# The mean of squares of eight head pairs: from TensorE to VectorE's transposes and sums

## The chip, the cores and the metric

One core of a Trainium2 chip runs the kernel. The time is device time in microseconds (us) of one execution; lower is better. TensorE (PE) does matrix products, VectorE (DVE) and ScalarE (ACT) element-wise work, GpSimd (POOL) almost nothing here, SyncE (SP) starts most transfers. Each engine works through its own queue in order and waits on semaphores where it needs another's result.

## The reference

An attention block without softmax feeds a two-layer network. Everything is float32 in and out.

```python
kv  = np.einsum('bhsd,bhse->bhde', k, v)            # 8 batches, 8 heads, 576 tokens, head size 64
out = np.einsum('bhsd,bhde->bhse', q, kv)
rms = np.sqrt(np.mean(out * out, axis=-1, keepdims=True) + 1e-06)
x   = (out / rms * g_norm)                          # then (b, s, h*d): 4608 tokens x 512
h   = x @ w_in                                      # 512 x 2048
g   = h * erf(softplus(h))
y   = g @ w_out                                     # 2048 x 512
```

The part that matters here is `np.mean(out * out, axis=-1)`: the mean over the 64 values of one head of one token.

## The kernel before, in words

The tokens are worked in nine groups of 512, T = 0 to 8. Group T below 8 holds the first 512 tokens of batch T; the 64 tokens that are left of each batch are collected in `x_last` and make the ninth group. A group's attention is worked in four pairs of heads, p = 0 to 3: two heads of 64 stand above one another on the 128 partitions, tokens lie along the free axis, so a result of a pair is 128x512. The network is worked by 16 units f of 128 of its 2048 hidden values: `h` for the unit (four TensorE products with one 128x512 weight tile in plain float32, or twelve with three fp32r forms of each operand: high, low and both), softplus, erf in batches of four units, the product h·s ("gate", L1082), and the projection by `w_out`.

**Three ways to do the norm.** The mean runs over partitions, which no element-wise engine sums. In the group T = 0 (`first_group`, L873) TensorE sums it with `mean_w`, a matrix with 1/64 in two 64x64 blocks. The groups T = 1 and T = 2 (`attention`, L404) do so too, and this is what the change touches. The pair (1,0) does it with two float32 products (L476). The other seven pairs first halve the squares into two fp32r numbers on VectorE (`halve`: L459 and L460) and make four fp32r products (L470, L471). Logarithm, exponential and square (L482 to L484) then give 1/rms on ScalarE, on 128x512 elements, since the products write the mean to all 64 rows of a head; VectorE adds a correction step (L490, L493) and multiplies the attention result by it (L502). The groups from T = 3 on (`paired`, L542) do two pairs at once and use no TensorE for it: VectorE transposes the squares in blocks of 32x32 (L629), so that 32 rows come to lie along the free axis, and sums them (L630). Each head then has two partial sums on different partitions. Four ScalarE copies (`across`, L643) bring each to the other's place, VectorE adds them (L644), logarithm, exponential and square run on 128x32 elements (L649 to L651), two small operations correct (L658, L661), and a transpose with a broadcast input (L665) spreads the result over 128x512 again.

**What sets the order.** The program is written under a manual schedule: each engine takes its instructions in the order in which Python issues them. The first group has a list of names (ORDER). Then a loop (L1156) runs over n = 0 to 32, units f of the groups T = 0 and T = 1; in it stand, at each step, the weight tiles still to be made from 64-bit inputs (`weights`, L309: ScalarE converts the lower halves, L271, VectorE does four operations, L281 to L292, the last of which writes the tile), the gate product of an earlier unit (L1175 or L1220), the hidden product of unit n, its evacuation from PSUM by ScalarE (L1214 for float32, L1216 for the fp32r forms, where VectorE adds the second bank, L753), its softplus (L1230) and the projection of the unit n-5 (L834). While the group T is in the network, the attention of the group T+1 is done a piece at a time. `pieces_of` (L1028) puts these pieces into four lists for each step f; the loop calls list 3 and list 0 ahead of the step's hidden product, list 1 after its softplus, list 2 at the end of the step. With T+1 = 1 the pairs begin at steps n = 3, 6, 9 and 12, with T+1 = 2 at n = 16, 20, 24 and 28; `halve` and the copies of the kept tail (`keep_tail`, L447: the 64 last tokens and the next pair's kv) run two steps later in list 3, `mean` in that step's list 1 (list 2 for pair (1,0)), `norm` one step later in list 0. The last pair, (2,3), has its `mean` and `norm` after the loop, in `held_sums` (L1110). While the group T = 1 is in the network, the weights are also split into three fp32r forms (L737, L740, L743) and written to DRAM, and the last four units' gated values are split into `g_held` (L713, L716, L719) for products at L1098. A second loop (L1323) does the remaining seven groups in fp32r, with the weight forms read back from DRAM (`w_in_parts`, `w_out_parts`).

PSUM: two banks (`ps_h`) take hidden products in turn, four (`ps_o`) the projections, and `at_ps` two banks the attention pieces of a pair.

Of the kernel before, what the change touches and what calls it, by code (L numbers as in the profile page):

```python
# [39 lines left out]
FP32 = mybir.dt.float32  # L40
# [8 lines left out]
EPS = 1e-6  # L49
# [21 lines left out]
def kernel(  # L71
# [41 lines left out]
    def exp_ln_table():  # L113
        nc.scalar.preload_act_table_set("natural_log_exp_and_others")
# [225 lines left out]
    def qt_tile(name):  # L340
        return attp.tile([P, S], FP32, name=name, tag="qT", bufs=2)
# [58 lines left out]
    def keep_prepared():  # L400
        kept.pop()()
        turn(1, 0)

    def attention(T, p):  # L404

        st = {}

        halves = T > 1 or (T == 1 and p > 0)
        then = divmod(T * NP + p + 1, NP)
        both = (T, p) == (FIRST, NP - 1)  # L410
        more_cols = slice(kv_cols.stop, kv_cols.stop + D)

        two = halves_of

        bd = kv_of(T, p)

        def square_tile(name):
            return qt_tile(name)[:, 0:G]

        def visit():  # L420


            qT = ready.pop((T, p))
            at = st["at"] = at_tile()
            x = halves_of(qT[:, 0:G])
            for a, i in ((0, 0), (0, 1), (1, 0), (1, 1)):
                nc.tensor.matmul(  # L427
                    at[rows_of[i if a else 1 - i], a, 0 : 2 * P],
                    lhsT=bd[rows_of[i], a * D : (a + 1) * D],
                    rhs=x[rows_of[i], a],  # L430
                    start=True,
                    stop=True,
                )
            for s in rows_of:
                nc.tensor.matmul(
                    at[s, 1, 2 * P : 2 * P + R], lhsT=bd[s, D : 2 * D], rhs=qT[s, G:S], start=True, stop=True
                )
            st["o"] = at[:, :, 0 : 2 * P]
            for _, product_ in kv_products(*then, at[:, 1, kv_cols], at[:, 0, kv_cols], first=1):
                product_()  # L440
            if both:
                for _, product_ in kv_products(then[0], 1, at[:, 1, more_cols], at[:, 0, more_cols]):
                    product_()
            st["sq"] = qT[:, 0:G]
            nc.scalar.activation(two(st["sq"]), st["o"], AF.Square)

        def keep_tail():  # L447
            nc.vector.tensor_copy(
# [3 lines left out]
            if both:  # L452
                kv_kept(then[0], 1, st["at"], more_cols)

        def halve():
            sq = st.pop("sq")
            hi = st["hi"] = attp.tile([P, G], FP32R, name="sq_hi", tag="rms_r")
            lo = st["lo"] = attp.tile([P, G], FP32R, name="sq_lo", tag="sq_lo")
            nc.vector.tensor_copy(out=hi, in_=sq)  # L459
            nc.vector.tensor_tensor(out=lo, in0=sq, in1=hi.bitcast(FP32), op=ALU.subtract)  # L460

        def mean(table=True):
            ms = st["ms"] = st["at"][:, :, 2 * P : 4 * P]
            parts = [(ms[:, a], a) for a in range(2)]
            if halves:


                hi, lo = two(st.pop("hi")), two(st.pop("lo"))
                for ps, a in parts:
                    nc.tensor.matmul(ps, lhsT=mean_w, rhs=hi[:, a], start=True, stop=False)  # L470
                    nc.tensor.matmul(ps, lhsT=mean_w, rhs=lo[:, a], start=False, stop=True)  # L471
                u = square_tile("u")
            else:
                u = st.pop("sq")
                for ps, a in parts:
                    nc.tensor.matmul(  # L476
                        ps, lhsT=mean_w.bitcast(FP32), rhs=two(u)[:, a], start=True, stop=True
                    )
            r = attp.tile([P, G], FP32, name="rms_r", tag="rms_r")
            exp_ln_table()  # L480
            st["u"], st["r"] = u, r
            nc.scalar.activation(two(r), ms, AF.Ln, bias=eps_col)  # L482
            nc.scalar.activation(r, r, AF.Exp, scale=-0.5)
            nc.scalar.activation(u, r, AF.Square)  # L484
            if table:
                softplus_table()

        def norm():
            ms, u, r = (st.pop(name) for name in ("ms", "u", "r"))
            nc.vector.scalar_tensor_tensor(  # L490
                out=two(u), in0=ms, scalar=EPS, in1=two(u), op0=ALU.add, op1=ALU.mult
            )
            nc.vector.scalar_tensor_tensor(  # L493
                out=u, in0=u, scalar=3.0, in1=r, op0=ALU.subtract, op1=ALU.mult
            )
            if T < FIRST:
                if T not in xT:
                    xT[T] = wide.tile([P, KC, G], FP32, name="xT", tag="ab"[T])
                x = xT[T][:, p, :]
            else:  # L500
                x = st["x"] = x_new.tile([P, G], FP32, name="x", tag="x")
            nc.vector.scalar_tensor_tensor(  # L502
                out=two(x),
                in0=st.pop("o"),
                scalar=gm_col,
                in1=two(u),
                op0=ALU.mult,
                op1=ALU.mult,
            )
# [23 lines left out]

        first_ = (partial(prepare, T, p),) if (T, p) == (1, 0) else ()
        then_ = partial(turn, *then)
        pieces = (first_, (visit, loads), (halve, keep_tail) if halves else (keep_tail,))
        return (*(partial(chain, *group) for group in pieces), mean, partial(chain, norm, then_), split)


    twice = {}  # L540

    def paired(T, p):  # L542
# [73 lines left out]
                twice["o", n] = o  # L616
                nc.scalar.activation(x, o, AF.Square, scale=0.125)

        def small(name):
            t = twice[name] = attp.tile([P, 2 * BLOCKS], FP32, name=name, tag=name)  # L620
            return t

        def block_sums():


            total = small("ms")
            for n in range(2):
                t = attp.tile([P, G], FP32, name="sq_t", tag=("rms_r", "sq_lo")[n])
                nc.vector.transpose(out=t, in_=twice["x"][n])  # L629
                nc.vector.tensor_reduce(  # L630
                    out=total[:, n * BLOCKS : n * BLOCKS + BLOCKS],
                    in_=t.rearrange("p (c d) -> p c d", c=BLOCKS),
                    axis=AX.X,
                    op=ALU.add,
                )

        def across():


            total, other = twice["ms"], small("ms_other")  # L640
            for n in range(4):
                rows, beside = (slice(32 * k, 32 * k + 32) for k in (n, n ^ 1))
                nc.scalar.copy(other[rows], total[beside])  # L643
            nc.vector.tensor_tensor(out=total, in0=total, in1=other, op=ALU.add)  # L644

        def root():
            total, r, u = twice["ms"], small("rms"), small("rms_u")
            exp_ln_table()
            nc.scalar.activation(r, total, AF.Ln, bias=eps_col)  # L649
            nc.scalar.activation(r, r, AF.Exp, scale=-0.5)  # L650
            nc.scalar.activation(u, r, AF.Square)  # L651
            softplus_table()

        def spread():


            total, r, u = (twice[name] for name in ("ms", "rms", "rms_u"))
            nc.vector.scalar_tensor_tensor(  # L658
                out=u, in0=total, scalar=EPS, in1=u, op0=ALU.add, op1=ALU.mult
            )  # L660
            nc.vector.scalar_tensor_tensor(  # L661
                out=u, in0=u, scalar=3.0, in1=r, op0=ALU.subtract, op1=ALU.mult
            )
            for n in range(2):
                nc.vector.transpose(  # L665
                    out=twice["x"][n].rearrange("p (c d) -> p c d", c=BLOCKS),
                    in_=u[:, n * BLOCKS : n * BLOCKS + BLOCKS].unsqueeze(2).to_broadcast([P, BLOCKS, 32]),
                )

        def norm(n):  # L670
            x = twice["x"][n]
# [356 lines left out]
    def pieces_of(T):  # L1028


        steps = [([], [], [], []) for _ in range(FC)]
        for p in range(NP):
            products, apply, halve, mean, norm, split = attention(T, p)
            f = (BATCH - 1) * (p + 1) if T < FIRST else BATCH * p

            steps[f][2 if T == FIRST or p == 1 else 1].append(products)
            if T < FIRST and p == 0:
                steps[f + 2][3].append(apply)
            else:
                steps[f + 1][1].append(apply)  # L1040
            steps[f + 2][3].append(halve)
            with_erf = (f + 2) % BATCH == BATCH - 1

            place = 2 if T < FIRST and p == 0 else 1
            if T == FIRST and p == NP - 1:
                ending.extend((partial(mean, table=False), norm, split))
                continue
            steps[f + 2][place].append(partial(mean, table=not with_erf))
            steps[f + 3][0].append(norm)
            steps[min(f + 4, FC - 1)][0].append(split)  # L1050
        return steps
# [400 lines left out]
```

## Time and profile before

| | |
|---|---|
| three runs: median (lowest to highest) | 885.0 us (884.7 to 885.28) |
| the profiled execution: time | 885.01 us |
| its span | 883.2 us |
| TensorE clock granted | 1.0 |
| ScalarE, busy share of the span | 63% |
| DMA, mean rate over the span | 294 GB/s |
| attention pieces of T = 1 lie from about | 41 us to 122 us |
| those of T = 2 from about | 134 us to 231 us |

The profile shows one execution. Its page lists the busy time of each engine and, in 40 equal slices of the span, the busy share in tenths. Further views of the same trace are the chain of waits (for each moment, what the work that ended last was waiting for), the timeline (start, duration, engine, line, operation and tile, and in brackets how long the engine stood idle before it and for whom), busy times of the engines in a stretch, and the durations of all instructions of a line (lowest/median/highest in ns, first and last start).

### The profile page before, as it was taken

Reading aid. Unit: us, or ns where it says so; the run is one execution under the profiler, and the core shown is the slowest. Engines: PE = TensorE matmul, PEld = TensorE weight load, DVE = VectorE, ACT = ScalarE, POOL = GpSimd, SP = SyncE. Lnnn points to the kernel's source line nnn. Section 1 sums busy time; section 2 is a strip of 40 time slices with the busy share of each in tenths; the row PEclk is TensorE's granted clock in tenths of the full one; section 3 lists DMA queues with packets and bytes.
Section 4 is the critical chain, followed back from the end, with each engine's and each line's share of the span. In section 5 each row is a group of like instructions: output and inputs, shape, how many; then the busy total and the mean of one; then the engine's idle time right before and its main releaser. Section 6 shows DMA issues by size and latency. Waiting matters only on the chain.

```text
span 883.2 us, 13286 instructions
## 1 busy us (share of the span) xinstructions
PE 875.1 (99%) x4874; PEld 659.1 (75%) x4874; DVE 752.6 (85%) x1107; ACT 559.3 (63%) x789; POOL 4.7 (1%) x14
## 2 busy tenths in 40 slices
PE   8999999999999999999999999999999999999998
PEld 4444456666788888888888888888888888888887
DVE  5889978899998898989898989898979797966667
ACT  5977677777775657565665647474757575755552
POOL 2000000000000000000000000000000000000000
PEclk9999999999999999999999999999999999999999
DMA  9977427989799997999799979998797779778871
GB/s 291 291 225 224 132 75 285 342 310 341 262 358 401 330 347 251 385 328 349 232 382 350 353 231 346 366 342 295 272 351 282 288 288 344 289 279 334 316 255 49
DMA packets 136929, 259.89 MB, mean 294 GB/s; under 512 B 78816, under 2 KB 87264, under 8 KB 136864
## 3 DMA queue, kind: packets, MB, share of 16 engines
q1 hardware_dynamic: 136128, 258.09, 82.8%
q10 hardware_dynamic: 544, 0.82, 0.3%
q8 instruction: 39, 0.64, 0.3%
q14 instruction: 26, 0.21, 0.1%
q0 software_dynamic: 192, 0.13, 0.0%
HBM read 224.40 MB, written 34.60 MB: 293 GB/s over the span
## 4 chain that ended last, share of the span: by engine, by line
PE 91%; DMA 3%; DVE 2%; ACT 2%; issue 1%; SPq 0%; DVEq 0%; ACTq 0%
PE n_ps L778 48%; PE m_ps L778 24%; PE o_ps L834 8%; PE h_ps L1201 5%; DMA w_out_parts<-w_out 1%; PE at_ps L557 1%; DMA q_sb<-in_q_dram 1%; PE off_ps L588 1%; DMA w_in<-w_new 1%; PE warm_ps L982 1%; DMA w_in_parts<-w_in 0%; PE at_ps L427 0%; ACT s_sb L1154 0%; PE at_ps L440 0%; ACT L1154 0%
## 5 line engine op out<-in xcount | busy, mean ns | idle before, releaser
L778 PE MATMUL n_ps<-w_out_parts,g_forms 128*128 128x512 f32 (+1 forms) x936 | 230.1, 388 | 0.2 <-DMA w_out_parts<-w_out 0.2
L778 PE MATMUL n_ps<-x_forms,w_in_parts 128*128 128x512 f32 x896 | 222.6, 390 | 0.0
L778 PEld LDWEIGHTS n_ps<-w_out_parts,g_forms 128*128 128x128 f32 x936 | 175.0, 188 | 36.7 <-DMA w_out_parts<-w_out 0.9
L778 PEld LDWEIGHTS n_ps<-x_forms,w_in_parts 128*128 128x128 f32 x896 | 167.4, 188 | 35.1
L753 DVE TENSOR_TENSOR h<-m_ps,h 128x512 f32<-128x512 f32 x116 | 78.5, 686 | 58.6 <-PE m_ps L778 58.5
L1358 ACT ACTIVATE h<-n_ps 128x512 f32<-128x512 f32 x112 | 66.7, 596 | 94.0 <-PE n_ps L778 91.8
L1363 ACT ACTIVATE s<-h 128x512 f32<-128x512 f32 x112 | 69.2, 632 | 88.6 <-DVE h L753 88.6
L778 PE MATMUL m_ps<-w_out_parts,g_forms 128*128 128x512 f32 x464 | 123.9, 389 | 0.0
L778 PE MATMUL m_ps<-x_forms,w_in_parts 128*128 128x512 f32 x448 | 119.7, 389 | 0.0
L778 PEld LDWEIGHTS m_ps<-w_out_parts,g_forms 128*128 128x128 f32 x464 | 87.1, 188 | 18.1
L778 PEld LDWEIGHTS m_ps<-x_forms,w_in_parts 128*128 128x128 f32 x448 | 84.1, 188 | 17.5
L753 DVE TENSOR_TENSOR e<-m_ps,e 128x512 f32<-128x512 f32 x116 | 80.1, 692 | 14.1 <-PE m_ps L778 3.4
L834 PE MATMUL o_ps<-w_out_sb,h_sb 128*128 128x512 f32 x192 | 86.8, 595 | 0.0
L713 ACT ACTIVATE g_forms<-h 128x1024 fp32r<-128x1024 f32 x58 | 60.8, 1061 | 39.2 <-PE m_ps L778 21.0
L719 DVE SCALAR_TENSOR_TENSOR g_forms<-g_forms 128x1024 fp32r<-128x1024 f32 x58 | 71.1, 1226 | 2.0
L716 DVE TENSOR_TENSOR g_forms<-h,g_forms 128x1024 fp32r<-128x1024 f32 x58 | 70.5, 1215 | 0.5 <-ACT g_forms L713 0.4
L1412 DVE TENSOR_TENSOR h<-h,s 128x1024 f32<-128x1024 f32 x56 | 65.9, 1217 | 0.0
L834 PEld LDWEIGHTS o_ps<-w_out_sb,h_sb 128*128 128x128 f32 x192 | 35.5, 190 | 38.3 <-issue 36.9
L748 DVE SCALAR_TENSOR_TENSOR e<-n_ps,e 128x512 f32<-128x512 f32 (+1 forms) x89 | 59.8, 671 | 3.4 <-PE n_ps L778 3.4
L1201 PE MATMUL h_ps<-xT,w_in_sb 128*128 128x512 f32 x128 | 57.9, 596 | 1.3 <-DVE w_in_sb L292 1.2
L117 ACT ACT_TABLE_LOAD x43 | 55.2, 1283 | 0.8
L1386 ACT ACTIVATE s<-s 128x1024 f32<-128x1024 f32 x50 | 50.6, 1054 | 0.3
(166 smaller groups left out, 936.6 us busy)
## 6 DMA issues: line engine op xcount, KB each, us to landing
w_out_parts<-w_out SPq DMA_DIRECT2D x116, 768.0 KB, 7.2
w_in_parts<-w_in SPq DMA_DIRECT2D x112, 768.0 KB, 6.7
w_in<-w_new SPq DMA_DIRECT2D x16, 768.0 KB, 4.8
k_sb<-in_k_dram SPq DMA_DIRECT2D x32, 288.0 KB, 6.1
v_sb<-in_v_dram SPq DMA_DIRECT2D x31, 288.0 KB, 5.7
w_raw<-in_moe_w_in_dram SPq DMA_DIRECT2D x16, 512.0 KB, 6.3
w_raw<-in_moe_w_out_dram SPq DMA_DIRECT2D x8, 1024.0 KB, 5.3
out_dram<-e SPq DMA_DIRECT2D x32, 256.0 KB, 4.0
```

What stands on the lines that cost most here:

```text
L117: nc.scalar.preload_act_table_set("softplus")
L713: nc.scalar.activation(high, x, AF.Copy, scale=1.0 + 2.0**-13)
L716: nc.vector.tensor_tensor(out=low, in0=x, in1=high.bitcast(FP32), op=ALU.subtract)
L719: nc.vector.scalar_tensor_tensor(out=both, in0=low.bitcast(FP32), scalar=SHIFT, in1=high.bitcast(FP32), op0=ALU.mult, op1=ALU.add,)
L748: nc.vector.scalar_tensor_tensor(out=out_, in0=ps, scalar=scale, in1=out_, op0=ALU.mult, op1=ALU.add)
L753: nc.vector.tensor_tensor(out=out_, in0=ps, in1=out_, op=ALU.add)
L778: nc.tensor.matmul(ps[:, cols], lhsT=weights(form, k), rhs=moving(form, k)[:, cols], start=(form == forms[0] and k == 0), stop=(form == fo ...
L834: nc.tensor.matmul(o_ps[j], lhsT=g[:, j * P : j * P + P], rhs=one(w_out_sb, f), start=(f == 0), stop=last,)
L1201: nc.tensor.matmul(plain[i], lhsT=blocks_of(one(w_in_sb, i % FC))[:, c], rhs=xT[T][:, c, :], start=(c == 0), stop=(c == KC - 1),)
L1358: nc.scalar.activation(h[:, i], n_ps, AF.Copy, scale=SHIFT - 1.0)
L1363: nc.scalar.activation(s[:, i], h[:, i], AF.Softplus)
L1412: nc.vector.tensor_tensor(out=part(h, half), in0=part(h, half), in1=part(s, half), op=ALU.mult)
```

## The change

In `attention` the mean goes the way that `paired` already goes. The steps of `paired` become functions that both call: `small`, `sums_of_blocks`, `meet`, `roots` and `spread_over`; for the groups from T = 3 on they issue what was issued before. For the eight pairs of T = 1 and T = 2, `halve`, the products with `mean_w`, and the three ScalarE and two VectorE operations on 128x512 go. In their place come: the transpose and the sum right behind the kept tail's copies (`block_sums`, list 3), the four copies and the add at once behind them (`across`, list 0 of the same step, so ahead of that step's hidden product and its evacuation), logarithm, exponential and square on 128x16 where `mean` stood, and two small operations, the spreading transpose and the multiplication where `norm` stood. The square takes a scale of 1/8, so that sums are means. The first group keeps its TensorE products. No transfer is added, removed or moved in SyncE's queue.

```diff
+    def sums_of_blocks(squares):
+        total = small("ms", len(squares))
+        for n, x in enumerate(squares):
+            t = attp.tile([P, G], FP32, name="sq_t", tag=("rms_r", "sq_lo")[n])
+            nc.vector.transpose(out=t, in_=x)
+            nc.vector.tensor_reduce(
+                out=total[:, n * BLOCKS : n * BLOCKS + BLOCKS],
+                in_=t.rearrange("p (c d) -> p c d", c=BLOCKS), axis=AX.X, op=ALU.add,
+            )
+        return total
+
+    def meet(total):
+        other = small("ms_other", total.shape[1] // BLOCKS)
+        for n in range(4):
+            rows, beside = (slice(32 * k, 32 * k + 32) for k in (n, n ^ 1))
+            nc.scalar.copy(other[rows], total[beside])
+        nc.vector.tensor_tensor(out=total, in0=total, in1=other, op=ALU.add)
...
     def attention(T, p):
...
-            nc.scalar.activation(two(st["sq"]), st["o"], AF.Square)
+            nc.scalar.activation(halves_of(st["sq"]), st["o"], AF.Square, scale=0.125)
...
-        def halve():
-            sq = st.pop("sq")
-            hi = st["hi"] = attp.tile([P, G], FP32R, name="sq_hi", tag="rms_r")
-            lo = st["lo"] = attp.tile([P, G], FP32R, name="sq_lo", tag="sq_lo")
-            nc.vector.tensor_copy(out=hi, in_=sq)
-            nc.vector.tensor_tensor(out=lo, in0=sq, in1=hi.bitcast(FP32), op=ALU.subtract)
-
-        def mean(table=True):
...
-                for ps, a in parts:
-                    nc.tensor.matmul(ps, lhsT=mean_w, rhs=hi[:, a], start=True, stop=False)
-                    nc.tensor.matmul(ps, lhsT=mean_w, rhs=lo[:, a], start=False, stop=True)
...
-            nc.scalar.activation(two(r), ms, AF.Ln, bias=eps_col)
-            nc.scalar.activation(r, r, AF.Exp, scale=-0.5)
-            nc.scalar.activation(u, r, AF.Square)
+        def block_sums():
+            st["ms"] = sums_of_blocks([st["sq"]])
+
+        def across():
+            meet(st["ms"])
+
+        def root(table=True):
+            st["r"] = roots(st["ms"], table)
...
-        pieces = (first_, (visit, loads), (halve, keep_tail) if halves else (keep_tail,))
-        return (*(partial(chain, *group) for group in pieces), mean, partial(chain, norm, then_), split)
+        pieces = (first_, (visit, loads), (keep_tail, block_sums), (across,))
+        return (*(partial(chain, *group) for group in pieces), root, partial(chain, norm, then_), split)
...
-            products, apply, halve, mean, norm, split = attention(T, p)
+            products, apply, keep, meets, mean, norm, split = attention(T, p)
...
-            steps[f + 2][3].append(halve)
+            steps[f + 2][3].append(keep)
+            steps[f + 2][0].append(meets)
```

## The prediction

> **What bounds the kernel now.** I began with the page's first two parts, busy time by engine and in 40 slices.
>
> ```profile
> PE 875.1 (99%) x4874; PEld 659.1 (75%) x4874; DVE 752.6 (85%) x1107; ACT 559.3 (63%) x789; POOL 4.7 (1%) x14
> ...
> PE   8999999999999999999999999999999999999998
> PEclk9999999999999999999999999999999999999999
> ```
>
> TensorE (PE) has work in 99% of the span and its clock is full in every slice. The average says that what leaves TensorE is a gain. But a gapless engine also has no slack to lend: any wait that is put in front of it is paid whole. So I read next, stage by stage, what stands just ahead of TensorE. By busy time per stretch, TensorE has 23.00 of the 23.50 us from 50.0 to 73.5, and VectorE (DVE) 22.60: there VectorE is as full as TensorE. From 73.5 to 118.4 TensorE has every microsecond, VectorE 41.80 of 44.90. The chain of waits around the first two pairs concerned (start, us, what):
>
> ```profile
> 45.73 0.22 DVE x_last L448
> ...
> 46.79 0.70 DVE w_e L281
> ...
> 49.51 1.24 DVE w_in_sb L292
> 50.74 0.04 issue
> 50.78 3.70 PE h_ps L1201 x8
> ...
> 69.59 0.12 PE at_ps L470
> 69.71 0.12 PE at_ps L471
> 69.82 0.12 PE at_ps L470
> 69.94 0.12 PE at_ps L471
> 70.06 3.43 PE o_ps L834 x8
> ```
>
> The reader is to see two things. Before 50.78 the chain runs on VectorE without a break: the kept tail of pair (1,0), then the four operations that make a weight tile, then TensorE, which the timeline shows standing still for that tile. From there on the chain is TensorE's own, and the four mean matmuls of a pair are 4 x 0.12 = 0.47 us of it.
>
> ```profile
> 50.78 3.70 PE L1201 MATMUL h_ps<-xT,w_in_sb 128*128 128x512 f32 x8 [0.50 <-DVE w_in_sb L292]
> ```
>
> **What goes.** On TensorE: seven pairs x 0.47 = 3.29 us, all of it in the gapless chain (69.59, 92.03, 114.47, 141.7, 168.5, 195.4, 222.04), and 1.03 us of L476 for pair (1,0) at 49.26. The latter stands before the 0.50 us stall above, and the stall ends when VectorE ends; it counts for nothing. On VectorE, per pair: L459 0.43, L460 0.69, L490 0.69, L493 0.69 = 2.50 (pair (1,0): 1.38). On ScalarE (ACT): L482 to L484, 0.69 + 0.63 + 0.63 = 1.95.
>
> **What comes.** The third and later groups do the same operations already, so the prices are rows of the trace:
>
> ```profile
> L643 ACT COPY ms_other<-ms x48: 213/217/219, 250.4 to 751.3; 32x32 f32<-32x32 f32 x48
> L629 DVE STREAM_TRANSPOSE sq_t<-x x24: 701/702/703, 246.4 to 747.9; 128x512 f32<-128x512 f32 x24
> L630 DVE TENSOR_REDUCE ms<-sq_t x24: 685/686/687, 247.1 to 748.7; 128x16 f32<-128x512 f32 x24
> ```
>
> VectorE: transpose 0.70, reduce 0.69, the add of the two halves 0.18 (L644), two small products 0.18 and 0.19 (L658, L661), the spreading transpose 0.69 (L665) = 2.63 per pair. In total that is no more than before (+0.13), except for pair (1,0), +1.25. ScalarE: four copies 0.90 (at 250.45, one group), then 0.32 + 0.23 + 0.23 for logarithm, exponential and square = 1.68 against 1.95. The rows for the small ones are of 128x32 and 32x32, the change has half that width: between nothing and these rows. I take the rows, since a transpose of 128x512 and a copy of 32x32, sixty-four times apart in size, differ by a factor of three only.
>
> A rule stands against cutting ScalarE's work this small: the Trainium skill, "VectorE: DVE Perf Modes", section "The TRN2 errata — SBUF-src ops pay a fixed extra latency per instruction", gives ScalarE a fixed cost of 224 cycles for each operation within SBUF and says that many small tiles pay it each. By it a 32x16 copy would be an estimated 200 ns, so four of them 0.80 us where the trace's group has 0.90; the sum would be smaller by some 0.1 us at a place where a pair waits for them.
>
> So busy time is a wash, and the order decides. Before, the squares went to TensorE and VectorE was free of the pair until the logarithm came back, several microseconds later. Now VectorE's add waits for ScalarE's copies, which wait for VectorE's reduce, and both queues run in order: behind the add stand the weight tiles and the gate products, behind the copies stands the evacuation of the hidden product's bank.
>
> **Step 1, pair (1,0).** The kept tail starts at 45.73 and ends at 46.79. Then transpose and reduce, to 48.21; ScalarE is busy with nothing that must come first after the square that ends at 45.70, so its copies run 48.25 to 49.15; the add; and L281 starts at 49.30 where it started at 46.79. The tile's join L292 ends 2.5 us later and TensorE stands for it: **+2.5**. Bounds: +1.4, if the copies cost no wait (transpose and reduce remain), and +3.0, if the two hand-overs to ScalarE and back take 0.25 each more than the 0.04 allowed here (the square's, at 45.70, took 0.03).
>
> **Step 2, pairs (1,1) to (1,3).** TensorE loses 3 x 0.47 = **-1.41**. VectorE: pair (1,1)'s copies stand in ScalarE's queue behind a batch of erf with its two table loads:
>
> ```profile
> 66.72 1.28 ACT L117 ACT_TABLE_LOAD   x1
> 68.02 1.16 ACT L271 ACTIVATE w_m<-w_raw 128x1024 int32<-128x1024 uint32 x1
> ```
>
> They come where L271 stands: 68.02, with the 2.5 us of step 1 70.5, done at 71.4. The next L281, at 65.37 before, starts at 71.57: VectorE is 6.2 us late, TensorE 2.5 - 0.47 = 2.0. The idle 0.38 ahead of L490 at 74.23 and the cheaper end of the pair (1.06 for 1.38) give back 0.7. The gate product that a projection needs ends at 81.66, the projection (L834) starts at 84.97: 3.3 us of cover against a lag of 5.5 - 2.0 = 3.5: a wait of about 0.2. Pairs (1,2) and (1,3) stall VectorE 1.0 each (four copies and two hand-overs; the add follows the reduce at once). Cover at the next two: gate 104.46, projection 107.41, 2.95; gate 123.61, projection 125.24, 1.63. By the same count 1.5 and 1.2 are waited there. Sum 2.9; none, if idle stretches of VectorE that I haven't seen pass (3.1 us of 44.9 are idle from 73.5 to 118.4) absorb it. Between 0 and 2.9 I take **+2.3**, nearer to the count, since TensorE's own shortening eats the cover too.
>
> **Step 3, pairs (2,0) to (2,2).** No stall: in these steps two weight tiles' splits (L740, L743) stand between reduce and add. The copies precede the evacuation L1216, but would end at 140.7 for a product that ends at 140.9, and with 1.3 and 0.6 us to spare at the other two. So 3 x 0.47 = **-1.41**. If they don't fit: up to +0.3 each.
>
> **Step 4, pair (2,3).** This step has no projection between two hidden products, so TensorE waits for the bank that L1216 empties:
>
> ```profile
> 218.22 0.22 DVE L448 COPY x_last<-at_ps 128x64 f32<-128x64 f32 x1
> 218.53 0.60 ACT L1216 ACTIVATE h<-n_ps 128x512 f32<-128x512 f32 x1 [0.37 <-PE n_ps L778]
> 219.25 0.42 PE L778 MATMUL n_ps<-x_high,w_new 128*128 128x512 f32 x1
> ...
> 222.90 1.18 PE L1098 MATMUL o_ps<-w_place,g_held 128*128 128x512 f32 x4 [0.23 <-DVE g_held L719]
> ```
>
> Without L459 and L460 the kept tails run from 217.15 to 219.2 (two kv sums here), transpose and reduce to 220.6, the copies to 221.5, the evacuation to 222.1: the product of L778 starts at 222.16, not 219.25, +2.9. Less the mean, 0.47, and the two later waits for g_held (0.23 and 0.15), which the delay covers: **+2.05**. Bounds: -0.47 (copies fall behind the evacuation) to +2.45.
>
> **Sum**: 2.5 - 1.41 + 2.3 - 1.41 + 2.05 = +4.0. After 225 TensorE is the chain to the end and the DMA has spare time on the whole, so the shift stays, less at most the 0.2 us that TensorE waits for w_out_parts near 242. The profiled execution took 885.01 us (span 883.2, 1.8 around it, untouched), the median of the runs shown is 885.0: **889.0 us**.
>
> **The rivals.**
> **Only the matmuls count (faster).** If the copies come through without any wait for TensorE, the gain is 3.29: 881.7. Point from which it decides: the new operations of pair (1,0) must cost VectorE under about 0.5 us before 50.7, and the last pair's copies must be out before 218.5. The tail ends at 46.79 and the tile follows without a gap, and the last pair's squares are done only at 217.1, 1.4 us ahead of the evacuation, with 0.70 + 0.69 needed before the first copy: this speaks against. For it: TensorE is 99% busy, and the work that leaves it is certain.
> **Cover holds in the middle (hardly slower).** Steps 1 and 4 cost as counted, but VectorE's lag never reaches TensorE: 2.5 - 2.82 + 2.05 = +1.7, 886.7. For it: cover of 3.3, 2.95 and 1.63 us; against: VectorE has 93% of that stretch.
> **The lag adds up (much slower).** Step 2 at its upper end 2.9, the copies of (2,0) to (2,2) past the evacuation by 0.3 each: +5.5, 890.5.
> **It does not do what it says.** The order of instructions on TensorE shows 29 rows fewer, so the matmuls do go; that the time stays at 885 by waits that happen to equal the gain needs steps 1 and 4 half as large.
>
> **How the numbers follow.** The forecast has 0.62, the large lag 0.15, the covered middle 0.12, no change by cancelling 0.04, faster 0.07. About 0.2% (1.8 us) is what a measurement of this kernel can tell from no change, so 886.7 is still "within": faster 0.07, same 0.16, slower 0.77. Range 886.4 to 890.8: it leaves out the faster case, the cancelling one and the ends of steps 1 and 3 together.
>
> **What would show it.** Right: TensorE idle of some 2.5 to 3 us ahead of h_ps near 50 to 53, put down to w_in_sb; a VectorE idle of 2 to 4 us ahead of the small add of pair (1,1); idle ahead of two or three L834 projections put down to the gate product h_sb; idle of nearly 3 us ahead of n_ps near 220. Wrong: if any of these is missing, its term goes; if TensorE's busy time does not fall by about 4 us, the gain side was misread; if the time is lost after 242, the DMA was the cause and not the queues.

## The result, and the profile after

The changed kernel takes 892.8 us (median of four executions, 892.58 to 894.54), the kernel before 885.02. The ratio is 1.0092, 95% interval [1.0075, 1.0110]: slower by 7.8 us. The forecast was slower by 4.0, and the measured time lies above the range that was given (886.4 to 890.8).

The profiled execution of the changed kernel is its slowest one: 894.54 us, span 892.7. Its first 46 us hold 0.9 us that are no part of the change: TensorE there waits 1.1 us for a query transfer (`q_sb`), before the first changed instruction; in the profiles of other kernels here that wait is absent or shorter, whatever their code. Shifts below are told with that 0.9 taken off.

The page's first two parts, as they were shown of before:

```profile
PE 874.8 (98%) x4842; PEld 656.9 (74%) x4842; DVE 754.6 (85%) x1125; ACT 556.9 (62%) x821; POOL 4.7 (1%) x14
...
PE   8989989999899999999999999999999999999998
PEclk9989999999999999999999999999999999999999
```

TensorE has 32 instructions less, and yet its busy time hardly fell, from 875.1 to 874.8. One digit gives the hint: the granted clock, all nines before, has an 8 in the third slice. Instructions that run there at a lower clock are longer, and they are counted as busy. The row is coarse: a nine stands for anything from 90% up over 22 us, and a second fall, near 230 us, doesn't change its digit. The longest of TensorE's waits, from 23 to 260 us (engine and line, what it waited for, us in total, times, longest):

```profile
PE h_ps L1180 <- ACT rms L435: 3.9, 1, 3.9
PE o_ps L812 <- DVE h_sb L1061: 2.9, 2, 1.5
PE n_ps L756 <- ACT h L1195: 2.7, 1, 2.7
```

These are the three places that the prediction named, with waits of the sizes that it named. The first, in the timeline (start, duration, engine, line, operation, in brackets the idle time before it and who ended it):

```profile
49.19 0.84 ACT L428 COPY ms_other<-ms 32x16 f32<-32x16 f32 x4 [2.56 <-DVE ms L414]
...
50.06 0.18 DVE L429 TENSOR_TENSOR ms<-ms,ms_other 128x16 f32<-128x16 f32 x1 [0.91 <-ACT ms_other L428]
50.16 0.69 DVE L281 TENSOR_SCALAR w_e<-w_raw 128x1024 f32<-128x1024 f32 x1
...
52.87 1.23 DVE L292 CUSTOM_DVE_ANT_0 w_in_sb<-w_e,w_m 128x2048 uint16<-128x2048 uint16 x1
...
54.24 6.38 PE L1180 MATMUL h_ps<-xT,w_in_sb 128*128 128x512 f32 x8 [3.89 <-ACT rms L435]
```

Two things are to be read. VectorE stands 0.91 us ahead of its add, then makes the weight tile, which is done at 54.10; TensorE starts right after. (The profile names the exponential L435 as releaser because that ended at 54.23; experiments below, with the exponential elsewhere, name `w_in_sb`; in e3_dve_copies it ended 3.4 us earlier, and the product starts 0.14 us behind the tile, as here.) And the eight products then take 6.38 us, where the same eight took 3.70 in the profile before. Busy time by stretch (stretch, length, TensorE, its weight loads, VectorE, ScalarE, GpSimd, granted clock, DMA share, GB/s):

```profile
50.00:60.00 10.00, 6.11 (x8) 2.48 (x8) 9.52 (x14) 6.75 (x10) 0.00 (x0) 0.66 0.58 185
```

The granted clock is 0.66 in the mean over these 10 us; from 60 to 78 it is 1.00 again. In steps of 0.1 us it is half from 52.86, still within the wait, to 59.68:

```profile
52.86:59.68 6.82, 5.44 (x7) 2.37 (x8) 6.54 (x9) 3.97 (x6) 0.00 (x0) 0.50 0.81 259
230.35:233.76 3.41, 3.41 (x10) 2.63 (x9) 2.67 (x5) 1.80 (x4) 0.00 (x0) 0.50 1.09 320
```

The second row belongs to the third wait, which has the same sequel:

```profile
227.65 0.84 ACT L428 COPY ms_other<-ms 32x16 f32<-32x16 f32 x4 [2.47 <-DVE ms L414]
228.52 0.60 ACT L1195 ACTIVATE h<-n_ps 128x512 f32<-128x512 f32 x1
...
229.17 0.50 PE L756 MATMUL n_ps<-x_high,w_new 128*128 128x512 f32 x1 [2.73 <-ACT h L1195]
...
230.48 0.63 PE L756 MATMUL n_ps<-x_low,w_new 128*128 128x512 f32 x1
```

The evacuation L1195 stands behind the four copies, as forecast, and TensorE behind it. One microsecond after it goes on, its products turn from 0.39 to 0.63 us. The waits of the middle stage (L812 for the gate product `h_sb`, 1.46 and 1.41 us) have no such sequel: the eight products after each take 3.70:

```profile
114.19 3.70 PE L812 MATMUL o_ps<-w_out_sb,h_sb 128*128 128x512 f32 x8 [1.46 <-DVE h_sb L1061]
...
133.03 3.70 PE L812 MATMUL o_ps<-w_out_sb,h_sb 128*128 128x512 f32 x8 [1.41 <-DVE h_sb L1061]
```

By TensorE's own starts, the shift of each stage against the profile before (0.93 taken off; each entry is the difference of two starts):

| | us |
|---|---|
| wait ahead of the product at 54.24 | +2.53 |
| its lower clock, 6.38 in place of 3.70 | +2.67 |
| means of (1,1) to (1,3) gone | -1.41 |
| waits for the gate product, 0.13 + 1.53 + 1.56 | +3.2 |
| hand-overs up to the first product of pair (2,0) | +0.53 |
| means of (2,0) to (2,2) gone | -1.46 |
| wait ahead of the product at 229.17 | +2.90 |
| its lower clock (the 12 products, from start to start: 2.79 to 4.30) | +1.51 |
| mean of (2,3), waits for g_held gone | -1.27 |
| sum, at 245 us | +9.2 |

By the end of the span 8.6 are left (892.7 - 883.2 - 0.9). The median of the four executions, 7.8, is lower still, and so is their loss of clock: the profiled one has a mean granted clock of 0.994, the other three 0.995 to 0.996.

### The profile page after: what moved, and what is told of

Its sections match the earlier page's. It is cut to its first block, busy times and chain, and to the rows that moved or that the text cites. A ratio compares the mean times of both kernels' runs of the same rounds, so it can differ in the third digit from the quotient of the medians.

```text
span 892.7 us, 13259 instructions
## 1 busy us (share of the span) xinstructions
PE 874.8 (98%) x4842; PEld 656.9 (74%) x4842; DVE 754.6 (85%) x1125; ACT 556.9 (62%) x821; POOL 4.7 (1%) x14
## 4 chain that ended last, share of the span: by engine, by line
PE 87%; DVE 5%; ACT 5%; DMA 2%; issue 1%; SPq 0%; DVEq 0%; ACTq 0%
PE n_ps L756 50%; PE m_ps L756 25%; PE o_ps L812 5%; PE h_ps L1180 3%; DVE w_e L287 1%; PE at_ps L574 1%; PE off_ps L605 1%; PE n_ps L1077 1%; DMA q_sb<-in_q_dram 1%; ACT s_sb L1133 1%; DVE w_e L284 1%; ACT L117 1%; DMA w_raw<-in_moe_w_out_dram 1%; DVE w_e L281 1%; ACT L1133 0%
## 5 line engine op out<-in xcount | busy, mean ns | idle before, releaser
L812 PE MATMUL o_ps<-w_out_sb,h_sb 128*128 128x512 f32 x192 | 87.1, 596 | 2.9 <-DVE h_sb L1061 2.9
L812 PEld LDWEIGHTS o_ps<-w_out_sb,h_sb 128*128 128x128 f32 x192 | 35.9, 190 | 43.4 <-issue 37.8
L1180 PE MATMUL h_ps<-xT,w_in_sb 128*128 128x512 f32 x128 | 60.5, 619 | 4.6 <-ACT rms L435 3.9
L1180 PEld LDWEIGHTS h_ps<-xT,w_in_sb 128*128 128x128 f32 x128 | 24.9, 198 | 37.1 <-issue 29.4
```

Source lines behind the costliest of these rows:

```text
L812: nc.tensor.matmul(o_ps[j], lhsT=g[:, j * P : j * P + P], rhs=one(w_out_sb, f), start=(f == 0), stop=last,)
L1180: nc.tensor.matmul(plain[i], lhsT=blocks_of(one(w_in_sb, i % FC))[:, c], rhs=xT[T][:, c, :], start=(c == 0), stop=(c == KC - 1),)
```

## The experiments

**Theory A**: the two long waits are what the prediction said, order and hand-overs, but each is paid a second time, since TensorE runs at a lower clock after it. **Theory B**: the clock falls there for another reason. **Theory C**: it is not the place; VectorE's and ScalarE's new work costs this time wherever it stands.

### e1_fill: the same waits, but TensorE not idle in them

```diff
+        def fills(count):
+            for n in range(count):
+                nc.tensor.matmul(
+                    st["at"][:, n % 2, 2 * P : 4 * P],
+                    lhsT=mean_w.bitcast(FP32),
+                    rhs=halves_of(st["sq"])[:, n % 2],
+                    start=True,
+                    stop=True,
+                )
...
         def root(table=True):
+            if (T, p) == (1, 0):
+                fills(6)
```

and `fills(4)` for (2,3) behind the hidden product of step 30.

> The changed kernel with idle TensorE time filled: six 128x256 float32 products with mean_w (0.51 us each by L476) go where pair (1,0) had its mean, four go behind the hidden product of step 30; they write the unused part of at_ps, their result is read by nothing. No wait of VectorE or ScalarE is touched. Theory A (each of the two long waits is paid twice, once as a wait and once because TensorE's clock is lower after it): h_ps at 54.24 takes 3.7 instead of 6.38 us and the products after 229.17 go at full clock; 892.8 - 2.7 - 1.7 = 888.4, and the remaining waits of TensorE are as long as before less the fill. Theory B (the clock is low there for another reason, such as the power of VectorE's work): 892.8 as before, both clock dips stay. If the fill is longer than the wait: above 888.4 by the excess.

889.31 us; 885.31 before on the same chip; ratio 1.0046 [1.0030, 1.0063]. The timeline of e1_fill at the two places:

```profile
49.27 2.75 PE L509 MATMUL at_ps<-qT,mean_w 128*128 128x256 f32 x12
53.22 3.70 PE L1196 MATMUL h_ps<-xT,w_in_sb 128*128 128x512 f32 x8 [1.19 <-DVE w_in_sb L292]
...
225.09 0.50 PE L771 MATMUL n_ps<-x_high,w_new 128*128 128x512 f32 x1 [0.77 <-ACT h L1211]
```

The product starts when the tile is there, as late as in the changed kernel, but takes 3.70. The granted clock is 1.00 over both places (49 to 61 and 200 to 260 us). Useless work on TensorE made the kernel 3.5 us faster. Theory B is out; what is left, +4.0 against its own before, is waits and missing matmuls alone, the quantity that the prediction had worked out. The time is 0.9 above the 888.4 expected, which took the clock loss of the profiled execution, the slowest, off the median.

### e7_fill_4_0, e8_fill_2_4, e11_fill_6_0: how long a wait, and which of the two

The same edit with other counts at the two places.

> The changed kernel with four filling products of 0.5 us at pair (1,0) alone, none at (2,3); as in e1_fill their result is read by nothing. TensorE's idle time at (1,0) falls from 3.9 to some 2.0 us, that at (2,3) stays 2.7. Theory A, if 2.0 us of idle leave the clock: h_ps takes 3.7 and only the second dip stays: 889.3 + 1.0 to 1.7 = 890.3 to 891.0. If the clock falls after 2.0 us too: 892.8. Theory B: 892.8.

> As e1_fill, but two filling products at pair (1,0), as many as the mean that was removed there, and four at (2,3). TensorE's idle time at (1,0) is then some 2.9 us, at (2,3) 0.8. If the clock falls after 2.9 us as it did after 2.7 at (2,3): h_ps takes over 5 us, 889.3 + 2.2 to 2.7 = 891.5 to 892.0. If it does not: 889.3, and the removal of that mean's two products was by itself what cost the clock there.

> The changed kernel with six filling products at pair (1,0), none at (2,3), so that only the wait of 2.7 us at (2,3) can lower the clock; many runs. In e7_fill_4_0 two of four executions took about 889 and two 892 to 894, after the same wait in the profile. If the clock after such a wait falls in some executions and not in others: two groups again, one near 889.3 (mean granted clock 0.999 or 1.0), one 2 to 4 us above (0.996). If it is a matter of the four fills' place alone: one group near 889.3 to 891.

e8_fill_2_4: 891.0 us, ratio 1.0068 [1.0054, 1.0081]. Two products, as many as the mean that had been taken away, leave a wait of 2.93 us, and the clock falls (the time is 0.5 below the 891.5 to 892.0 expected):

```profile
52.86 5.40 PE L1196 MATMUL h_ps<-xT,w_in_sb 128*128 128x512 f32 x8 [2.93 <-DVE w_in_sb L292]
```

e7_fill_4_0: 890.76 us, ratio 1.0076 [1.0057, 1.0095], but the four executions lie in two groups: 888.94 and 889.25 at a mean clock of 0.999, 892.28 and 893.69 at 0.996. The median lies within the 890.3 to 891.0 expected, but no execution does. The profiled one is the first of them:

```profile
52.95 3.70 PE L1196 MATMUL h_ps<-xT,w_in_sb 128*128 128x512 f32 x8 [2.07 <-DVE w_in_sb L292]
```

```profile
224.81 0.50 PE L771 MATMUL n_ps<-x_high,w_new 128*128 128x512 f32 x1 [2.72 <-ACT h L1211]
...
226.74 1.08 PE L771 MATMUL m_ps<-x_both,w_new 128*128 128x512 f32 x4
```

Here a wait of 2.72 us at (2,3) left the clock whole: the four products of m_ps take 1.08, as they do before such a wait. e11_fill_6_0, with that wait alone: 890.97 us, ratio 1.0064 [1.0051, 1.0076], five executions from 890.12 to 891.23. They lie in one group by time, so the two groups of e7_fill_4_0 did not come again; one of them, 890.12, has a mean clock of 0.999 like two of e1_fill, so it may have kept its clock. In its profile the same 2.72 us are followed by the fall, within a microsecond:

```profile
225.66 0.50 PE L771 MATMUL n_ps<-x_high,w_new 128*128 128x512 f32 x1 [2.72 <-ACT h L1211]
...
226.22 0.48 PE L771 MATMUL n_ps<-x_high,w_new 128*128 128x512 f32 x1
226.50 0.63 PE L771 MATMUL n_ps<-x_low,w_new 128*128 128x512 f32 x1
```

So a wait of 2.72 us may or may not be paid twice. The traces say more about which. In steps of 0.1 us, the clock is half from 53.00 to 56.41 in e8_fill_2_4 and from 226.40 to 229.81 in e11_fill_6_0: 3.41 us, as at 230.35 in the changed kernel, whose first fall lasts 6.82, twice that. Its two falls begin 177.49 us apart, 52 times 3.413. So the clock looks as if it were set anew every 3.41 us, by how long TensorE stood idle in the step just over; a stretch at half clock then costs some 1.7 us. Idle time in the step ahead of the fall, by busy time: 2.23 and 2.51 us in the changed kernel, 2.93 in e8_fill_2_4, 2.68 in e11_fill_6_0:

```profile
222.98:226.40 3.42, 0.74 (x3) 0.66 (x4) 2.03 (x5) 1.44 (x6) 0.00 (x0) 1.00 1.00 392
226.40:229.81 3.41, 3.41 (x9) 2.65 (x9) 3.11 (x5) 2.23 (x4) 0.00 (x0) 0.50 1.09 336
```

Where the steps lie in e7_fill_4_0, which has no fall, can be estimated from the product at 4.16 us, the fourth of the trace. It takes 0.78 us in e11_fill_6_0 and 1.05 in the changed kernel, whose steps stand 0.54 later (230.35 less 226.40 less 3.41); 0.92 in e6_moved, whose steps stand 0.29 later (its half clock begins at 233.51). Both are twice the difference in duration, as if this product ran at half clock until one of the steps. (The clock row shows 1.00 there, so this is read from durations.) In e7_fill_4_0 it takes 0.81, so its steps would stand 0.06 later than in e11_fill_6_0, at 223.04 and 226.46:

```profile
4.16 0.81 PE L975 MATMUL warm_ps<-ones 128*128 128x512 f32 x1
```

Its gap, 222.09 to 224.81, is then cut into 0.95 and 1.77, where that of e11_fill_6_0, 222.94 to 225.66, lies in one step. This is worked out from the traces; no experiment moved a gap to test it. Against e1_fill (889.31) the second place costs 1.7 us in e11_fill_6_0, the first one 1.7 in e8_fill_2_4 at its shorter wait. Whether the executions of 892.28 and 893.69 us lost their clock at (2,3) alone isn't known, as only the profiled execution has a trace.

### e2_two_old and e4_three_new: which pairs cost

`attention_old` is the function of before, issued for the pairs named; the others are as changed.

```diff
-            products, apply, keep, meets, mean, norm, split = attention(T, p)
+            products, apply, keep, meets, mean, norm, split = (attention_old if (T, p) in OLD else attention)(T, p)
```

> The changed kernel, but pairs (1,0) and (2,3) take the mean by TensorE as before; the other six pairs are as changed. Theory A (the cost is order: waits at these two pairs, their clock dips, and a lag of VectorE at pairs (1,1) to (1,3)): both long waits and both dips go; left are -2.82 for six means, +3.2 for the waits of L812 for the gate product: 885 + 0.4 = 885.4, with TensorE waits on h_sb of some 3 us in sum. Theory C (VectorE's new work itself costs, wherever it is put): six eighths of the loss stay, 885 + 0.75 x 7.8 = 890.8. Theory D (the lag was only lent by pair (1,0)'s delay): 885 - 2.8 = 882.2.

885.48 against 885.31, ratio 1.0003 [0.9993, 1.0012]. Without (1,0) and (2,3) the loss is gone; theory C, which gave 890.8, falls. The gain of six means, 2.82 us, goes into the lag of VectorE:

```profile
PE o_ps L956 <- DVE h_sb L1205: 2.5, 2, 1.5
```

> Only pairs (2,0) to (2,2) as changed; the five others take the mean by TensorE as before. Theory A: three means leave a gapless TensorE, no wait comes: 885.0 - 1.41 = 883.6, with at most 0.3 lost per pair if the copies hold up the evacuation L1216. Theory C (the new VectorE work costs): 885 + 3/8 x 7.8 = 887.9. Rival: TensorE's gain is taken back later by the DMA: 885.0.

883.65, ratio 0.9980 [0.9971, 0.9990]. The three pairs of T = 2 are a plain gain of three times 0.47, as reckoned.

### e3_dve_copies: the way to ScalarE

```diff
-            nc.scalar.copy(other[rows], total[beside])
+            (copy or nc.scalar.copy)(other[rows], total[beside])
...
-            meet(st["ms"])
+            meet(st["ms"], nc.vector.tensor_copy if True else None)
```

The second call is that of the eight pairs; the later groups keep their copies on ScalarE.

> The changed kernel, but the four 32x16 copies of the eight pairs run on VectorE in front of the add, not on ScalarE. This adds work to VectorE (four small operations, some 0.4 to 0.7 us per pair) and takes away the way to ScalarE and back. Theory A (the hand-over through a queue in order is the cost): no stall ahead of the add; the evacuation ahead of n_ps near 220 to 229 is on time; TensorE still waits about 3.4 for w_in_sb near 50 to 54 and its clock falls there; lag of VectorE under 0.5: 892.8 - 0.5 - 2.9 - (2.9 - 0.7) - 1.7 = 885.5, between 884.5 and 887. Theory C (VectorE's work is the cost): slower than the changed kernel, 893 to 896.

888.18, ratio 1.0038 [1.0023, 1.0053]: 4.6 us faster than the change with more work on VectorE. Theory C is out a second time. The four copies take VectorE 0.70 (0.84 on ScalarE, plus the hand-overs), and no wait for the gate product is left. The longest waits of TensorE that remain, from 23 to 260 us:

```profile
PE h_ps L1180 <- DVE w_in_sb L292: 3.7, 1, 3.7
PE m_ps L756 <- DVE h L731: 0.9, 1, 0.9
PE o_ps L1077 <- DVE g_held L697: 0.7, 1, 0.7
```

The expectation, 885.5, was too low by 2.7: the wait at (1,0) fell by 0.14, not by 0.5, since four copies in a row on VectorE take almost as long as the detour, and the products behind it took 6.73 us, 0.35 more than in the changed kernel. The two shorter waits above, 0.9 and 0.7, stand at (2,3), where 0.4 had been before. Together that is 1.9 of the 2.7; the rest wasn't traced.

### e6_moved and e10_eight: the same operations in other places

In e6_moved the sums and copies of (1,0) are issued behind its step's weight tile, gate product and softplus, those of (2,3) at the end of step 31.

```diff
+        if (T, p) in ((1, 0), (FIRST, NP - 1)):
+            pieces = (first_, (visit, loads), (keep_tail,), (block_sums, across))
...
-            steps[f + 2][0].append(meets)
+            if (T, p) == (1, 0):
+                steps[f + 2][1].append(meets)
+            elif (T, p) == (FIRST, NP - 1):
+                steps[FC - 1][2].append(meets)
+            else:
+                steps[f + 2][0].append(meets)
```

> The changed kernel with the same operations for all eight pairs; only for (1,0) and (2,3) the transpose, sum, copies and add are issued later: for (1,0) behind the weight tile, the gate product and the softplus of its step, for (2,3) behind the last split for g_held, at the end of step 31. Theory A (place, not work): both long waits of TensorE and both clock dips go; the seven means count, -3.29; the waits for the gate product stay and may grow, since VectorE is as late as before and TensorE is not: 2.5 to 5: 884.2 to 886.7. Theory C (VectorE's and ScalarE's new work costs wherever it stands): 892.8.

888.41, ratio 1.0039 [1.0025, 1.0053], a miss by 1.7 us. At (1,0) it went as expected: a wait of 1.48 us (1.03 of it where the mean's products had been), then 3.67 for the eight products. At (2,3) the end of step 31 was too late. The logarithm and the normalisation run after it, and the evacuation of `e` stands behind them in ScalarE's queue:

```profile
232.64 0.60 ACT L1115 ACTIVATE e<-n_ps 128x512 f32<-128x512 f32 x1
...
233.29 5.54 PE L1084 MATMUL n_ps<-w_place,g_held 128*128 128x512 f32 x16 [2.84 <-ACT e L1115]
```

A new wait of 2.84 us, and again the products behind it are long: 5.54, where the same sixteen took 3.92 before. In e10_eight the sums of (2,3) stand at the end of step 30 instead (`steps[f + 2][2]`), and the copies of (2,3) and of the pairs of T = 1 run on VectorE.

> All eight pairs with block sums, none by TensorE: as e9_seven, and pair (1,0) with its sums behind the weight tile, gate product and softplus of step 5, copies on VectorE. Same arithmetic as the changed kernel, other places, and VectorE instead of ScalarE for the copies of five pairs. Theory A (place and hand-over, not work): TensorE idles 1.5 us at (1,0) instead of working 1.03 and idling 0.5, so nothing is gained there, the clock stays; VectorE's lag of 2.2 from this pair adds to that of the next three, so 0 to 2 us of waits for the gate product: 883 to 885, and faster or equal to before where the change was 0.9% slower. Theory C (the work costs): 890 or more.

885.38, ratio 1.0002 [0.9993, 1.0011]: all eight pairs without TensorE, the arithmetic of the change, and the time of before. The clock stays whole; the waits of TensorE are 1.5 for the tile, 1.8 for the gate product and 0.8 at (2,3), about what the matmuls gave. The upper end of the expectation was 885.

### e5_six_dve and e9_seven: can it win

> Six pairs as changed, (1,0) and (2,3) by TensorE as before (as in e2_two_old); in addition the copies of pairs (1,1) to (1,3) run on VectorE. Theory A (order): the kernel with the same six pairs and ScalarE copies took 885.5 with 2.5 us of waits for the gate product; without the way to ScalarE these waits go, as they went in e3_dve_copies: 885.0 - 2.82 = 882.2, at most 883. It would beat both kernels. If the waits stay: 885.5.

883.26, ratio 0.9980 [0.9971, 0.9989]: faster than both kernels. No wait for the gate product is left in its profile. The median gained 1.8 us where 2.8 were expected, and lies 0.3 above the 883 that was called the most; the profiled execution, whose product at 50.78 starts 0.75 later than in the profile before by its first stage alone, gained 2.0.

> Seven pairs with block sums, (1,0) by TensorE as before. As e5_six_dve, and pair (2,3) too: its transpose, sum, copies (on VectorE) and add are issued at the end of its own step 30, behind the first two units' g_held, so neither ahead of the evacuation (as in the change) nor too late for the logarithm (as in e6_moved, where they stood at the end of step 31 and a wait of 2.8 us came for the evacuation e). Theory A: e5_six_dve took 883.3; -0.47 for the mean, -0.38 for waits on g_held at the first units, +0.5 for the third unit's: 882.9, between 882.4 and 883.6, no wait of TensorE over 1 us. If any place in this stage costs a long wait: 885 to 888.

883.59, ratio 0.9986 [0.9977, 0.9994]: within what was expected, and no better than e5_six_dve; its wait at (2,3) is 0.8 us, so that pair returns its mean.

## Why the prediction was right and wrong

**What bounds the kernel**: right, and incomplete. "Any wait that is put in front of it is paid whole" is true, but it is not all that is paid.

**What goes and comes**: right. The prices of the third and later groups held at half width: transpose 0.70, reduce 0.69, add 0.18, spreading 0.71, the four copies 0.84, between the 0.90 taken and the other estimate there, 0.80.

**Step 1**: the wait was forecast as +2.5 and is +2.53. Its cost was not: 2.67 us more for the products after it. The removal of the pair's own products, which the text put at nothing, made this worse, since it turned 1.03 us of work into idle time just ahead of the stall: 3.89 us idle in all. With that much work put back (e8_fill_2_4) the eight products take 5.40 and not 6.38.

**Step 2**: -1.41 was right. The waits for the gate product were put at 2.3, with a count of 2.9; they are 3.2, of the same mechanism and in the places named (0.13, 1.53 and 1.56, against 0.2, 1.5 and 1.2). VectorE's stall ahead of the add of (1,1) was 3.15 us, as reckoned:

```profile
72.84 1.28 ACT L117 ACT_TABLE_LOAD   x1
74.14 0.84 ACT L428 COPY ms_other<-ms 32x16 f32<-32x16 f32 x4
...
75.01 0.18 DVE L429 TENSOR_TENSOR ms<-ms,ms_other 128x16 f32<-128x16 f32 x1 [3.15 <-ACT ms_other L428]
```

**Step 3**: right, -1.46 for -1.41, and e4_three_new shows it alone. **Step 4**: the wait was forecast as +2.9 and is +2.90; its sequel, 1.51 in the twelve products behind it, was left out.

**The failed step** is thus the price of a wait in steps 1 and 4: a stall of TensorE was taken to cost its length. The prediction read "its clock is full in every slice" as a property of the kernel, where it was a consequence of TensorE having no long gap. Without that second cost the forecast holds: e1_fill, which keeps every wait and only fills the idle time, takes 889.31, and 889.0 was forecast. The rest of the distance is the clock, 3.5 us between the medians of e1_fill and of the changed kernel, 4.2 by the starts in the profiled execution (2.67 and 1.51). That the sum agrees to 0.3 us is in part luck: the waits for the gate product were 0.9 longer than taken, the hand-overs of 0.53 were not in it, and some 0.6 of the shift is gone again between 245 us and the end.

Much of that could have been read beforehand. The Trainium skill, "TensorE: Matmul & The Clock Gate", section "Part 1: The HAM clock gate (the "warmup" mystery)", says that the array's clock is halved after an idle window of some 3.4 us, that the window runs freely, and that the effect therefore varies between runs; its section "Why this matters for your kernels" advises against idle gaps over about 3 us. The runs agree on the halving (a granted clock of 0.50; 0.23 us from start to start of the fp32r products before, 0.43 after the fall), on the variation, and on the 3.4 us, as the length of a stretch at half clock; but here gaps of 2.72 and 2.93 us were enough, since 2.23 us of idle time in one step of 3.41 lowered the clock. By the page's limit alone the gap at (2,3) would have been taken as safe.

Of the **rivals**, the large lag came nearest in time, for a reason it did not have: the waits of step 2 were only 0.3 above its count. In the signs to look for, "if TensorE's busy time does not fall by about 4 us, the gain side was misread" was wrong itself: the busy time fell by 0.3, and the gain side was right.

**What stays open**: the same 2.72 us of idle time lowered the clock in the profile of e11_fill_6_0 and not in that of e7_fill_4_0. The place of the gap in the steps of 3.41 us fits both, but that is an inference from the profiles alone, and where the two executions of e7_fill_4_0 above 892 us lost their time isn't known. In e10_eight the waits that its profile shows leave about 1 us of the gain unaccounted for, which is about what executions of one kernel differ by.

## What to carry to other kernels

Work taken off a gapless engine is worth its time only if what replaces it stands in no queue ahead of that engine's next operand: here the same operations for eight pairs were 0.9% slower or even, by place and by the engine of four small copies, and for six or seven pairs up to 0.2% faster. When a change makes TensorE wait more than 2 us at one place, allow for a loss of clock behind the wait, here 1.5 to 3 us where it came (it came after waits of 2.7 us and more, not every time), and count removed matmuls next to the wait as part of the gap. Read the clock row beside the busy row: a busy time that does not fall although instructions went is a sign of a lower clock, and then read the clock in short stretches, since one digit in 40 can hide a fall.

## What the runs showed of the hardware that was not expected

Idle time of TensorE just ahead of eight float32 products of 128x512, and what they took, by the profiles: 0.50 us, 3.70; 1.19, 3.70; 1.46, 3.70; 1.48, 3.67; 2.07, 3.70; 2.93, 5.40; 3.75, 6.73; 3.89, 6.38. After 2.72 to 2.84 us of idle time ahead of fp32r products the clock fell in three profiles and stayed in one, and where it fell after 2.7 it did so only 0.7 and 1.2 us after work had gone on. Each of the six stretches at half clock that the traces hold is 3.41 us long, or 6.82 to 6.83 at (1,0) in the changed kernel and in e3_dve_copies. In the 3.41 us ahead of a fall TensorE had been idle for 2.23 us or more.

Filling a gap with products that nothing reads was worth 3.5 us.

Four copies of 32x16 take VectorE 0.70 us and ScalarE 0.84: at this size the two engines differ little. e3_dve_copies gained 4.6 us by moving them, by the order of the queues and not by their 0.14 us.
